# Agent attention and a maxout feed-forward: more turns of queries by transposing DMA, issued in runs, with a fourth slot for four tile classes and a new instruction order

## The chip, the cores and the metric

One Trainium2 chip, one NeuronCore of it. The metric is the device time of one execution in microseconds (us), taken as the median of several runs. One further execution is run under the hardware profiler; the page and the trace come from it. Engines are named as in the profile: PE (TensorE matmul), PEld (TensorE weight load), DVE (VectorE), ACT (ScalarE), POOL (GpSimd), SP (SyncE, which issues the DMAs). "L592" is line 592 of the kernel.

## The reference

```python
def _attn_ref(q, k, v, agents):          # q, k, v: (4, 12544, 128); agents: (4, 49, 128)
    scale = 1.0 / np.sqrt(q.shape[-1])
    def sm(a, b):
        s = scale * (a @ b.transpose(0, 2, 1))
        e = np.exp(s - s.max(-1, keepdims=True))
        return e / (e.sum(-1, keepdims=True) + 1e-09)
    agent_v = sm(agents, k) @ v          # 49 agents gather the values of a batch
    return sm(q, agents) @ agent_v       # each query takes a mix of the agents

def _moe_ref(x, w1, w2, w3, w_out):      # x: (50176, 128); w1, w2, w3: (128, 768); w_out: (768, 128)
    h = np.maximum(np.maximum(x @ w1, x @ w2), x @ w3)
    return h @ w_out                     # float32
```

The attention's result, reshaped to 50176 rows, is the x of the second part.

## The kernel before, in words

**Algebra.** With 49 agents a batch, each query row is a mix of 49 vectors. So the kernel never forms x: it multiplies the 49 agent vectors by the weights once per batch (a tile G) and multiplies the query's exps by G. G holds the differences w3 - w1 and w2 - w1 (columns C31 and C21) and the product w1 @ w_out. Since max(x1, x2, x3) is x1 plus relus of differences, a group's hidden part is two matmuls (`hidden`, L558), a relu on ScalarE (L571) and a maximum on VectorE (L574) for five of six blocks of 128 hidden columns; for block FI = 4 ScalarE does two relus in its place (L565, L568). The output is `out_linear` (L582) plus `out_hidden` (L592) and is divided by the sum of the exps by `out_scale` on VectorE (L599).

**Tiles and stages.** A tile is 128 rows of 128. Queries come in 49 groups (`NQ`): 12 groups of 8 tiles for each of four batches, and group 48 with the 2 tiles left of each. Keys and values come in chunks of 9 tiles (the last of a batch is smaller). Batch 0's keys and values are done first, in a head of some 40 us, together with the weights; those of batches 1 to 3 are done chunk by chunk inside the groups that "host" them (`host_of`: batch 1 in groups 1 to 11, batch 2 in 12 to 22, batch 3 in 24 to 34).

**What a group of queries takes.** `ql` loads it (float32, 512 KB, L513), `qc` casts it to bf16 on POOL into a QB tile (L517), then it is turned (128x128 tiles transposed) into a QT tile. There are two ways: `qt` on TensorE (eight matmuls with the identity, L523) and `qe` on VectorE (L527, out of PSUM); or, for groups in `TURNED`, `qd`, one transposing DMA issued by SP (`turn_by_dma`, L454). Then `sc` (scores, L533), `ex` (exps on ScalarE, L539), `su` and `re` (sums and reciprocals, L545, L550), six times `u`, `a`, `v`, `x` (hidden, relu or maximum), twice `li`, six `p`, `ov` (output), and `st` (store, L607).

**What a hosted chunk takes.** `kl`, `vl` (loads, L325), `kc`, `vc` (casts on POOL to KB and VB tiles, L335), `kt` (a transposing DMA on SP from KB to a KT tile, L454), `ks` (scores, L359), `kx` (exps to an EK tile, L365), `kv` (values, L376), `va` (sum of values on VectorE, L465) and `ea` (sum of exps on POOL, L474). Batch 0's chunks are turned on TensorE instead (L342, L347).

**The weights.** `lwo` loads w_out (L389), `cwo` casts it on POOL (L405), `pl` multiplies w1 by it (L417); all of the output part needs this. `wm` (L382) are warm-up matmuls whose result is not used; `SPARE` is their number.

**Order and slots.** Nothing is scheduled when the kernel is built: the string `ORDER` lists every step, and each engine gets its steps in that order. A word such as `kt1.0/1` names the step and the slot of the tile that it makes. `SLOTS` says how many buffers a tile class has; a step that makes a tile waits until the readers of the tile that had the slot before are done. All DMAs but one are issued by SP in the order of the string, so a DMA that waits holds all behind it; at most eight of them are under way at a time, since each waits for the one eight places ahead.

Of the kernel before, what the change touches and what calls it, by code (L numbers as in the profile page):

```python
# [14 lines left out]
P, H, C, A, B, NT, GT, KT, NF = 128, 64, 128, 49, 4, 98, 8, 9, 6  # L15
# [16 lines left out]
SLOTS = {"UV": 3, "OM": 2, "LD": 13, "QB": 3, "KB": 3, "VB": 4, "KT": 3, "QT": 3, "EQ": 4, "EK": 4, "AS": 3,  # L32
# [8 lines left out]
class Plan:  # L41
# [614 lines left out]
v.0.0/0 kc1.1/2 x.0.0/4 u.0.2/1 gvl v.1.5/2 a.0.2/1 li.0.0/0 kt1.1/2 p.0.0.3 x.1.5/5 p.0.0.1 ex.2/2 u.1.3/0 v.0.2/1 a.1.3/2
p.0.0.5 kt1.2/0 x.0.2/6 ks1.0/1 p.0.0.0 u.1.2/2 kx1.0/1 v.1.3/0 vc1.0/0 a.1.2/0 kl1.3/5 p.0.0.4 x.1.3/7 u.2.5/1 vl1.2/3 p.0.0.2
a.2.5/1 su.1 kl1.4/11 kv1.0 qc.3/0 u.1.1/2 ov.0.0/0 ql.5/9 v.1.2/0 a.1.1/2 vl1.4/2 u.1.4/1 re.1/1 va1.0/0 x.1.2/8 li.0.1/0 qt.3/1
kl1.8/8 vc1.1/0 a.1.4 p.0.1.4 u.1.0/2 qe.3/0 v.1.1/0 qc.4/0 a.1.0/0 v.1.4 x.1.1/2 p.0.1.1 vl1.3/4 p.0.1.5 p.0.1.3 x.1.4/0 p.0.1.2
p.0.1.0 u.2.3/0 ov.0.1 u.2.4/2 a.2.3/2 v.1.0/1 ks1.1/1 x.1.0/4 li.1.0/0 p.1.0.2 a.2.4 su.2 p.1.0.3 p.1.0.5 re.2/0 v.2.5/0 kx1.1/0  # L660
u.2.1/1 v.2.4 x.2.5/6 a.2.1/0 p.1.0.4 kv1.1 p.1.0.1 p.1.0.0 x.2.4/3 va1.1 v.2.1/0 ov.1.0/1 v.2.3/1 vc1.2/0 sc.3/1 x.2.3/1 u.2.2/2
ex.3/0 li.1.1/0 p.1.1.4 kc1.3/1 a.2.2/1 p.1.1.2 x.2.1/0 ks1.2/1 p.1.1.0 v.2.2/1 kx1.2/3 kc1.4/2 u.2.0/2 kt1.3/0 p.1.1.5 x.2.2/4
a.2.0/2 kv1.2 su.3 p.1.1.1 p.1.1.3 kl1.5/11 u.3.5/0 re.3/2 va1.2 v.2.0/1 ov.1.1 vl1.5/5 a.3.5/1 u.3.1/2 li.2.0/1 ql.6/3 x.2.0/7
p.2.0.3 p.2.0.4 kl1.6/6 a.3.1/0 qt.4/0 ql.7/10 u.3.4/0 qe.4/0 kt1.4/2 u.3.3/1 a.3.4 v.3.5/2 p.2.0.5 x.3.5/2 p.2.0.2 p.2.0.0
a.3.3/2 vc1.3/0 p.2.0.1 kl2.1/12 sc.4/0 ov.2.0/2 v.3.4 ex.4/1 v.3.3/2 ea1.0/0 v.3.1/1 x.3.4/5 x.3.3/8 li.2.1/1 vl2.0/7 p.2.1.5
ks1.3/0 su.4 p.2.1.4 kx1.3/1 x.3.1/6 u.3.2/0 u.4.5/2 a.3.2/2 kv1.3 p.2.1.3 kc1.5/1 p.2.1.0 va1.3 re.4/1 v.3.2/1 a.4.5/0 u.3.0/0
x.3.2/7 li.3.0/0 qc.5/0 p.3.0.5 kt1.5/0 a.3.0/1 p.2.1.2 p.2.1.1 u.4.3/2 ov.2.1 ea1.1 v.3.0/1 a.4.3/2 u.4.4/0 vl1.7/9 x.3.0/0
# [196 lines left out]
```

## Time and profile before

| | us |
|---|---|
| median of 3 runs | 447.99 (447.82 to 449.09) |
| the profiled execution | 448.96 |
| its span, first to last instruction | 447.1 |
| DVE maxima L574, 245 of 1219 ns | 293.4 busy |
| ACT relus L571, 245 of 1024 ns | 246.3 busy |
| PE hidden L558 and output L592 | 181.7 and 180.4 busy |
| DVE evictions of turned queries L527, 22 of 684 ns | 15.0 busy |
| PE turns of queries L523, 176 of 228 ns | 14.4 busy |

Busy time is the time in which an engine executes; idle time is split by what ended it. Matmuls are pipelined, so a busy PE may still be waiting. A line of the timeline has start, duration, engine, line, operation, tiles and count, and in brackets the idle time before it and who ended it. The granted clock of TensorE is 1.00 at full speed; the share of DMA is the mean over 16 engines of the time that their packets took, which can exceed 1 when packets overlap.

Transposing DMAs have no size in the profile's issue list; there are 33 of keys (KT<-KB, median 7.0 us from issue to landing) and 27 of queries (QT<-QB, 6.5 us).

### The profile page before, as it was taken

To read this page: it belongs to the slowest core of one execution; us is meant where nothing else is said; L and a number is where in the kernel's file an instruction comes from. 1 tells how busy PE (TensorE), PEld (TensorE's weight loads), DVE (VectorE), ACT (ScalarE), POOL (GpSimd) and SP (SyncE) were. 2 spreads that over 40 slices of the span, in tenths; PEclk is the share of its full clock that TensorE was granted. 3 is DMA by queue.
4 is the path that set the end of the run, shared out by engine and by line. 5 is a ranking of instruction groups with operands and counts; after the bars stand their busy time and mean duration, and the time that the engine had idled before them with its cause. 6 is when DMAs were issued, how large, how long until landed. Compare 5 with 4: busy or idle time off the path is not lost.

```text
span 447.1 us, 12853 instructions
## 1 busy us (share of the span) xinstructions
PE 421.8 (94%) x5260; PEld 270.8 (61%) x5260; DVE 392.1 (88%) x496; ACT 393.6 (88%) x461; POOL 169.5 (38%) x176
## 2 busy tenths in 40 slices
PE   0787899999999999999899999999999999999996
PEld 0554466666666666666566666666665555655675
DVE  1345799999999999999899999998999999999996
ACT  1469799999999999999889999999999999999983
POOL 1641645555694222824871324527601201000000
PEclk9989699999999999999999999999999999999999
DMA  8999999999999999999999999999699464450405
GB/s 312 410 408 387 346 372 281 298 405 308 327 291 307 352 285 285 345 310 225 321 354 253 313 302 345 303 221 353 189 300 282 103 189 122 90 195 22 164 37 202
DMA packets 97045, 121.98 MB, mean 273 GB/s; under 512 B 70423, under 2 KB 73179, under 8 KB 96987
## 3 DMA queue, kind: packets, MB, share of 16 engines
q1 hardware_dynamic: 96784, 121.07, 90.4%
q8 instruction: 41, 0.67, 0.6%
q14 instruction: 17, 0.14, 0.1%
q10 hardware_dynamic: 203, 0.10, 0.1%
HBM read 78.74 MB, written 25.69 MB: 234 GB/s over the span
## 4 chain that ended last, share of the span: by engine, by line
PE 83%; DMA 8%; DVE 3%; issue 2%; POOL 2%; ACT 1%; SPq 1%; DVEq 0%; POOLq 0%
PE UV L558 35%; PE OM L592 31%; PE OM L582 6%; DMA LD<-in_v_dram 4%; PE OM L533 3%; DVE R L574 2%; PE OM L523 2%; DMA LD<-in_k_dram 2%; PE OM L376 2%; PE OM L359 2%; DMA LD<-in_q_dram 1%; PE OM L545 1%; SPq L325 1%; DVE OS L599 1%; POOL QB L517 1%
## 5 line engine op out<-in xcount | busy, mean ns | idle before, releaser
L574 DVE TENSOR_TENSOR R<-UV,AS 128x1024 bf16<-128x1024 f32 x245 | 293.4, 1219 | 17.8 <-PE UV L558 12.9
L571 ACT ACTIVATE AS<-UV 128x1024 bf16<-128x1024 f32 x245 | 246.3, 1024 | 17.8 <-PE UV L558 13.5
L558 PE MATMUL UV<-EQ,G 49*128 49x512 bf16 (+1 forms) x1248 | 181.7, 371 | 0.9
L592 PE MATMUL OM<-wo_bf,R 128*128 128x128 bf16 x2352 | 180.4, 220 | 0.0
L592 PEld LDWEIGHTS <-R 128*128 128x128 bf16 x2352 | 139.8, 98 | 43.4 <-issue 41.1
L558 PEld LDWEIGHTS <-G 49*128 49x128 bf16 x1248 | 61.5, 94 | 61.8 <-issue 21.7
L517 POOL CAST QB<-LD 128x1024 bf16<-128x1024 f32 x49 | 51.1, 1048 | 98.4 <-DMA LD<-in_q_dram 50.3
L335 POOL CAST KB<-LD 128x1152 bf16<-128x1152 f32 (+2 forms) x45 | 49.7, 1116 | 60.4 <-DMA LD<-in_k_dram 42.8
L599 DVE TENSOR_TENSOR OS<-OM,RC 128x512 f32<-128x512 f32 x98 | 67.1, 684 | 3.6 <-PE OM L592 2.5
L335 POOL CAST VB<-LD 128x1152 bf16<-128x1152 f32 (+1 forms) x33 | 37.3, 1137 | 47.7 <-DMA LD<-in_v_dram 14.7
L565 ACT ACTIVATE UV<-UV 128x1024 f32<-128x1024 f32 x49 | 49.8, 1017 | 2.5 <-PE UV L558 1.2
L568 ACT ACTIVATE R<-UV 128x1024 bf16<-128x1024 f32 x49 | 50.1, 1023 | 1.7 <-PE UV L558 1.2
L582 PE MATMUL OM<-G,EQ 128*128 128x256 bf16 x196 | 37.9, 276 | 0.0
L539 ACT ACTIVATE EQ<-OM 128x512 bf16<-128x512 f32 x49 | 29.5, 602 | 0.9 <-PE OM L533 0.6
L474 POOL TENSOR_TENSOR EA<-EA,EK 128x441 f32<-128x441 f32 x27 | 27.6, 1023 | 4.8 <-ACT EK L365 4.1
L347 DVE COPY KT<-UV 128x1152 bf16<-128x1152 bf16 (+1 forms) x12 | 8.2, 700 | 17.3 <-PE UV L342 17.3
L582 PEld LDWEIGHTS <-EQ 128*128 128x128 bf16 x196 | 12.6, 97 | 15.6 <-issue 14.2
L533 PE MATMUL OM<-QT,agT 128*64 128x512 bf16 (+1 forms) x104 | 20.4, 398 | 0.2 <-DMA QT<-QB 0.2
L365 ACT ACTIVATE EK<-OM 128x441 bf16<-128x441 f32 (+1 forms) x33 | 17.8, 540 | 2.9 <-POOL EA L474 1.6
L376 PE MATMUL OM<-EK,VB 128*128 128x49 bf16 x392 | 17.3, 186 | 2.7 <-ACT VB L333 1.4
L359 PEld LDWEIGHTS <-KT 128*128 128x128 bf16 x392 | 14.6, 98 | 7.5 <-issue 4.5
L376 PEld LDWEIGHTS <-VB 128*128 128x128 bf16 x392 | 14.3, 97 | 7.9 <-issue 5.0
(67 smaller groups left out, 186.1 us busy)
## 6 DMA issues: line engine op xcount, KB each, us to landing
LD<-in_q_dram SPq DMA_DIRECT2D x48, 512.0 KB, 6.4
out_dram<-OS SPq DMA_DIRECT2D x48, 512.0 KB, 5.6
LD<-in_k_dram SPq DMA_DIRECT2D x40, 576.0 KB, 7.3
LD<-in_v_dram SPq DMA_DIRECT2D x40, 576.0 KB, 8.7
LD<-in_k_dram SPq DMA_DIRECT2D x3, 512.0 KB, 9.0
LD<-in_v_dram SPq DMA_DIRECT2D x3, 512.0 KB, 8.1
LD<-in_moe_w_dram SPq DMA_DIRECT2D x6, 192.0 KB, 8.4
KT<-KB SPq DMA_TRANSPOSE x33, 7.0
```

The costliest lines, as they stand in the source:

```text
L335: (self.nc.gpsimd if eng == POOL else self.nc.vector).tensor_copy(out=out, in_=src)
L376: self.nc.tensor.matmul(out, vb[:, j, :], e[:, j * A:(j + 1) * A], start=False, stop=True, skip_group_check=True)
L517: return lambda: self.nc.gpsimd.tensor_copy(out=self.t[f"qb.{s}"], in_=self.t[f"q.{s}"][:, :GT, :])
L533: self.nc.tensor.matmul(self.t[f"qs.{s}"][h * H:(h + 1) * H, jj * P:(jj + pairs) * P], self.agT[:, b, :], self.t[f"qT.{s}"][:, 2 * jj + h: ...
L558: self.nc.tensor.matmul(t[:, h, jj * P:(jj + pairs) * P], self.t[f"G{b}"][h * H:h * H + A, c + f * P:c + (f + 1) * P], self.t[f"e.{s}"][h ...
L565: return lambda: self.nc.scalar.activation(self.t[f"u.{s}.{f}"], self.t[f"u.{s}.{f}"], AF.Relu)
L568: return lambda: self.nc.scalar.activation(self.t[f"r.{s}.{f}"], self.t[f"u.{s}.{f}"], AF.Relu)
L571: return lambda: self.nc.scalar.activation(self.t[f"a.{s}.{f}"], self.t[f"u.{s}.{f}"], AF.Relu)
L574: return lambda: self.nc.vector.tensor_tensor(out=self.t[f"r.{s}.{f}"], in0=self.t[f"v.{s}.{f}"], in1=self.t[f"a.{s}.{f}"], op=ALU.max)
L582: self.nc.tensor.matmul(self.t[f"o.{s}.{o}"][:, i * 2 * C:(i + 1) * 2 * C], self.t[f"e.{s}"][:, jj * P:(jj + 1) * P], self.t[f"G{of[jj]}"] ...
L592: self.nc.tensor.matmul(self.t[f"o.{s}.{o}"][:, c:c + C], self.t[f"r.{s}.{f}"][:, h, jj * P:(jj + 1) * P], self.wo_bf[:, f, :], start=Fals ...
L599: self.nc.vector.tensor_tensor(out=self.t[f"os.{s}"][:, j:j + 4, :], in0=self.t[f"o.{s}.{o}"].rearrange("p (j c) -> p j c", c=C), in1=self ...
```

## The change

Four edits, three of them of constants:

- `TURNED` holds all groups from 13 to 48, 36 in place of 27. Groups 14, 16, 18, 20, 22, 24, 28, 30 and 34, which were turned on TensorE and evicted by VectorE, are turned by a transposing DMA on SP.
- QB, KB, KT and QT have four slots each in place of three.
- `SPARE` is 7: one warm-up matmul fewer.
- `ORDER` is new throughout. On SP the transposing DMAs stand in runs: the 69 of them form 24 runs, of up to ten, where 60 formed 43. w_out's load (`lwo`) stands directly behind the load of the second group's queries (`ql.1`), ahead of the first keys of batch 1 (`kl1.0`), where it stood behind those. In the head all of batch 0's keys tend to come before its values.

```diff
-SPARE = 8
+SPARE = 7
...
-TURNED = (*range(13, 36, 2), 26, 32, *range(36, 49))
+TURNED = range(13,49)
...
-SLOTS = {"UV": 3, "OM": 2, "LD": 13, "QB": 3, "KB": 3, "VB": 4, "KT": 3, "QT": 3, "EQ": 4, "EK": 4, "AS": 3,
+SLOTS = {"UV": 3, "OM": 2, "LD": 13, "QB": 4, "KB": 4, "VB": 4, "KT": 4, "QT": 4, "EQ": 4, "EK": 4, "AS": 3,
          "R": 13, "RC": 4, "OS": 9, "G": 4, "VA": 2, "EA": 2, "ES": 2, "KR": 2}
```

The steps on SP, taken out of the two strings, around the end of the head:

```
before: lw2b ql.1 kl1.0 lwo ql.2 kl1.2 ql.4 kl1.1 kt1.0 vl1.0 ql.3 vl1.1 kt1.1 kt1.2 kl1.3 ...
after:  lw2b ql.1 lwo kl1.0 ql.2 kl1.3 ql.3 kl1.1 kl1.2 vl1.1 vl1.0 kt1.0 kt1.1 kt1.3 kt1.2 kl1.9 ...
```

and in groups 16 to 19:

```
before: ql.22 vl2.9 ql.21 qd.19 kt2.7 kl3.1 st.8 vl3.0 vl3.2 kt2.8 kl3.0 vl3.1 kt2.9 qd.21 ql.24 st.14 vl3.5 st.13 kt2.10 kl3.2 ...
after:  ql.24 ql.21 ql.33 ql.22 st.3 st.11 qd.19 kt2.7 qd.20 kt2.8 kt2.9 kt2.10 qd.22 qd.23 kt3.1 qd.21 vl3.5 kl3.8 st.14 ql.29 ...
```

TensorE's steps around the product with w_out:

```
before: u.0.5 qt.1 v.0.1 u.0.4 pl v.0.5 sc.1 v.0.4 qt.2 u.0.0 v.0.3 u.1.5 sc.2 gl ...
after:  u.0.4 v.0.1 qt.1 u.0.3 pl v.0.5 v.0.4 sc.1 v.0.3 gl u.0.0 qt.2 u.1.5 v.0.0 ...
```

More of the change, by code (lines that the diff above doesn't have):

```diff
@@ L720 @@
-u.18.3/0 a.18.3/0 v.17.2/2 x.17.2/5 p.16.1.3 u.17.0/1 a.17.0/1 kt2.8/2 p.16.1.2 kv2.6 va2.6 p.16.1.0 ov.16.1 u.18.5/0 a.18.5/2
-v.17.0/2 u.18.4/1 x.17.0/8 su.18 li.17.0/0 p.17.0.5 p.17.0.3 a.18.4 p.17.0.2 re.18/2 u.18.1/0 v.18.5/2 kl3.0/10 a.18.1/1 v.18.4
-x.18.5/9 p.17.0.1 p.17.0.4 p.17.0.0 x.18.4/6 sc.19/1 qc.22/1 vl3.1/9 ov.17.0/0 v.18.3/0 v.18.1/2 ex.19/1 u.18.2/1 x.18.3/4 vc2.7/2
-li.17.1/0 a.18.2/2 p.17.1.3 p.17.1.0 ks2.7/1 x.18.1/8 su.19 p.17.1.1 kx2.7/3 u.19.5/1 v.18.2/0 a.19.5/0 p.17.1.2 x.18.2/1 u.18.0/2
@@ new lines @@
+u.19.3/0 v.18.0/1 a.19.3/2 u.19.4/2 vl3.5/11 qc.25/3 x.18.0/7 li.18.0/1 p.18.0.1 kl3.8/7 su.19 p.18.0.4 a.19.4 st.14 p.18.0.2
+ea2.7 re.19/1 u.19.1/0 ql.29/6 va2.7 v.19.5/1 a.19.1/0 kl3.0/12 v.19.4 kc3.4/3 x.19.5/4 p.18.0.3 vl3.8/0 p.18.0.5 p.18.0.0
+x.19.4/9 kl3.2/5 sc.20/0 ov.18.0/3 v.19.1/0 v.19.3/1 ex.20/2 st.8 u.19.2/2 x.19.1/6 li.18.1/1 a.19.2/1 ks2.8/0 p.18.1.5 p.18.1.4
+x.19.3/3 su.20 u.20.5/0 kx2.8/1 v.19.2/2 vc3.5/2 ql.28/1 p.18.1.1 a.20.5/0 p.18.1.0 re.20/0 x.19.2/2 u.19.0/1 p.18.1.2 a.19.0/2
@@ new lines @@
+ov.19.1 v.20.0/2 a.21.4 u.21.5/1 ql.26/12 x.20.0/8 su.21 li.20.0/0 p.20.0.3 p.20.0.1 a.21.5/0 p.20.0.2 kl3.5/10 qc.28/1 re.21/1
+v.21.4 v.21.5/2 x.21.4/2 u.21.1/1 x.21.5/3 p.20.0.5 ea2.9 p.20.0.4 ql.32/4 p.20.0.0 a.21.1/2 sc.22/1 ov.20.0/5 fo2/0 v.21.1/0
+v.21.3/2 ex.22/1 qd.24/3 u.21.2/1 x.21.1/9 li.20.1/0 a.21.2/0 p.20.1.4 ks2.10/1 p.20.1.3 x.21.3/7 v.21.2/0 qd.29/0 vc3.0/3
+kx2.10/0 u.22.5/1 p.20.1.5 a.22.5/2 kv2.10 x.21.2/5 u.21.0/2 kt3.0/2 to2 a.21.0/1 su.22 p.20.1.2 re.22/2 u.22.3/1 va2.10 nr2/0,2
@@ new lines @@
+v.21.0/0 a.22.3/0 u.22.4/2 kt3.4/1 x.21.0/4 p.20.1.1 p.20.1.0 li.21.0/1 a.22.4 p.21.0.5 p.21.0.1 qd.25/1 ov.20.1 v.22.5/0 u.22.1/1
+v.22.4 x.22.5/8 a.22.1/1 p.21.0.3 p.21.0.4 kl3.3/11 p.21.0.2 p.21.0.0 x.22.4/6 v.22.1/0 ov.21.0/0 sc.23/0 v.22.3/1 kl3.9/1
+x.22.1/0 ex.23/2 u.22.2/2 li.21.1/1 a.22.2/2 su.23/0 p.21.1.5 p.21.1.1 x.22.3/1 st.15 u.23.5/0 v.22.2/2 a.23.5/1 p.21.1.2 p.21.1.0
+re.23/0 x.22.2/5 gpl2/0 gpa2/1 gvl2 gpc2/0 qc.26/0 gva2 sc.24/0 gvc2 u.22.0/2 p.21.1.3 a.22.0/2 kc3.5/0 p.21.1.4 vl3.1/12 u.23.3/0
@@ new lines @@
+sc.25/1 x.23.0/5 li.23.0/0 qd.27/1 vc3.1/3 p.23.0.3 a.24.4 p.23.0.2 v.24.5/1 u.24.1/0 ex.25/1 x.24.5/2 kc3.2/1 p.23.0.5 p.23.0.4
+a.24.1/2 p.23.0.1 p.23.0.0 v.24.4 kc3.8/2 ov.23.0/8 kt3.2/2 v.24.1/1 u.25.5/0 x.24.4/8 x.24.1/1 li.23.1/1 p.23.1.0 ea3.0/0
+p.23.1.5 a.25.5/1 kt3.3/3 v.24.3/2 u.24.2/1 x.24.3/7 qc.32/3 p.23.1.2 a.24.2/2 ks3.1/0 vl3.9/7 su.25 v.24.2/0 vc3.2/0 ql.34/5
+re.25/2 u.24.0/2 kx3.1/0 x.24.2/6 st.18 p.23.1.4 p.23.1.3 a.24.0/0 kl3.6/4 kv3.1 p.23.1.1 va3.1 u.25.1/1 ql.38/2 ov.23.1 v.24.0/0
@@ new lines @@
+a.25.1/2 v.25.5/2 x.24.0/9 sc.26/0 kl3.10/12 li.24.0/1 p.24.0.2 ex.26/2 u.25.3/1 x.25.5/0 p.24.0.5 kl3.7/8 a.25.3/0 p.24.0.0
+p.24.0.4 u.25.2/0 vl3.4/11 v.25.3/1 a.25.2/1 u.25.4/2 x.25.3/4 p.24.0.1 p.24.0.3 a.25.4 li.24.1/0 p.24.1.0 u.26.5/0 ov.24.0/7
+v.25.1/1 a.26.5/0 v.25.4 x.25.1/9 p.24.1.4 ks3.2/1 p.24.1.3 x.25.4/8 su.26 v.25.2/0 re.26/0 u.25.0/1 x.25.2/7 kx3.2/1 p.24.1.1
+p.24.1.5 a.25.0/2 p.24.1.2 kv3.2 ov.24.1 u.26.4/2 v.25.0/0 a.26.4 u.26.3/1 x.25.0/6 li.25.0/0 p.25.0.1 p.25.0.5 a.26.3/1 p.25.0.3
@@ new lines @@
+kc3.6/3 v.26.4 va3.2 v.26.5/0 x.26.4/2 sc.27/1 x.26.5/1 qc.30/2 p.25.0.0 ql.31/4 p.25.0.4 p.25.0.2 st.23 ex.27/0 u.26.1/2
+ov.25.0/3 u.26.2/1 ql.36/6 a.26.1/0 v.26.3/0 kt3.5/2 ks3.3/1 x.26.3/5 li.25.1/0 p.25.1.2 a.26.2/2 v.26.1/2 p.25.1.0 qd.30/1
+x.26.1/7 p.25.1.5 kx3.3/3 u.26.0/1 v.26.2/0 a.26.0/1 kv3.3 su.27 x.26.2/0 kt3.6/3 u.27.5/2 p.25.1.4 a.27.5/0 p.25.1.1 p.25.1.3
+va3.3 re.27/1 u.27.4/0 ov.25.1 v.26.0/1 a.27.4 u.27.3/2 qc.31/1 x.26.0/4 sc.28/1 li.26.0/0 p.26.0.5 a.27.3/2 p.26.0.2 ea3.1
```

350 lines of the change are left out of this document (165 added, 185 removed).

## The prediction

> **What bounds the kernel now.** I read the page first (busy shares and chain), then the stretches between the exps of neighbouring groups, then the timelines of the two places where TensorE stands still, and last the DMA rate in steps of 1 us.
>
> The page: busy time, and the chain by engine.
>
> ```profile
> PE 421.8 (94%) x5260; PEld 270.8 (61%) x5260; DVE 392.1 (88%) x496; ACT 393.6 (88%) x461; POOL 169.5 (38%) x176
> ...
> PE 83%; DMA 8%; DVE 3%; issue 2%; POOL 2%; ACT 1%; SPq 1%; DVEq 0%; POOLq 0%
> ```
>
> TensorE carries the chain, but its busy time holds waits inside pipelined matmuls. So I look at one group at a time: busy time by stretch, from one group's exps to the next. Columns: stretch and length, then PE, PEld, DVE, ACT, POOL busy, TensorE clock, DMA share, GB/s.
>
> ```profile
> 165.10:173.10 8.00, 8.00 (x110) 5.29 (x108) 7.54 (x11) 7.79 (x10) 2.50 (x3) 1.00 1.12 353
> ...
> 181.30:189.40 8.10, 8.10 (x112) 5.52 (x109) 7.97 (x11) 7.88 (x11) 7.08 (x7) 1.00 1.09 350
> 189.40:197.30 7.90, 7.90 (x104) 5.03 (x101) 7.35 (x10) 7.68 (x11) 3.23 (x3) 1.00 1.13 278
> ...
> 213.50:222.90 9.40, 8.26 (x110) 5.35 (x108) 7.99 (x11) 7.68 (x10) 8.14 (x8) 1.00 1.06 324
> 288.40:296.30 7.90, 7.90 (x104) 5.26 (x101) 7.11 (x10) 7.63 (x11) 0.09 (x1) 1.00 1.17 224
> 296.30:304.20 7.90, 7.90 (x104) 5.04 (x100) 7.45 (x10) 7.65 (x10) 5.00 (x5) 1.00 1.08 314
> ```
>
> The first two stretches hold a turn of queries on TensorE and its eviction on VectorE (L523, L527), the third and the last two do not: theirs came by DMA. VectorE has 0.4 to 0.6 us less to do there, ScalarE the same 7.6 to 7.9 us, and the stretch is hardly shorter. ScalarE, idle 0.2 to 0.3 us in a group, sets the pace with the back-and-forth through three UV slots. The stretch from 213.5 is a stall of 1.4 us.
>
> **The head.** TensorE's timeline:
>
> ```profile
> 45.44 0.49 PE L417 MATMUL OM<-wo_bf,w1T 128*128 128x128 bf16 x6 [1.05 <-POOL wo_bf L405]
> ```
>
> GpSimd's timeline, and the stretches around it (columns as above):
>
> ```profile
> 44.56 0.83 POOL L405 CAST wo_bf<-LD 128x768 bf16<-128x768 f32 x1 [1.39 <-DMA LD<-in_moe_w_out_dram]
> ```
>
> ```profile
> 43.40:47.10 3.70, 2.46 (x24) 1.10 (x21) 2.56 (x4) 2.79 (x5) 2.54 (x3) 1.00 1.02 402
> 47.10:50.50 3.40, 2.98 (x18) 1.24 (x18) 2.12 (x3) 2.41 (x4) 1.93 (x3) 0.50 1.18 262
> 50.50:54.00 3.50, 3.50 (x24) 1.60 (x20) 2.64 (x3) 2.36 (x4) 1.96 (x3) 0.51 1.03 404
> ```
>
> TensorE waits for w_out, is busy 2.46 of 3.70 us, and then has 0.50 of its clock for two stretches.
>
> **The stall.** GpSimd's timeline, then ScalarE's:
>
> ```profile
> 212.34 1.14 POOL L335 CAST KB<-LD 128x1152 bf16<-128x1152 f32 x1 [4.27 <-DMA KT<-KB]
> ...
> 215.52 2.12 POOL L474 TENSOR_TENSOR EA<-EA,EK 128x441 f32<-128x441 f32 x2
> ```
>
> ```profile
> 216.57 0.54 ACT L365 ACTIVATE EK<-OM 128x441 bf16<-128x441 f32 x1 [1.55 <-POOL EA L474]
> ```
>
> A key cast waits 4.27 us for one of three KB slots, which a late transposing DMA still reads; two value casts and the sum of exps queue behind it, and ScalarE waits for the EK slot that this sum frees.
>
> **The DMA queue.** Stretches with POOL busy, clock, DMA share, GB/s:
>
> ```profile
> 200.00:201.00 1.00, 0.00 (x0) 1.00 1.04 417
> ...
> 203.00:204.00 1.00, 1.00 (x2) 1.00 0.38 45
> 204.00:205.00 1.00, 0.51 (x1) 1.00 0.25 59
> ...
> 210.00:211.00 1.00, 0.00 (x0) 1.00 0.12 6
> ```
>
> and the hosting stage beside the early one without transposes (all engines, columns as at first):
>
> ```profile
> 60.00:318.00 258.00, 256.26 (x3317) 167.36 (x3314) 244.31 (x307) 243.97 (x287) 130.72 (x134) 1.00 1.08 310
> 15.00:30.00 15.00, 12.63 (x176) 9.71 (x177) 6.49 (x11) 8.46 (x13) 8.37 (x9) 0.89 1.03 408
> ```
>
> Copies move 400 to 440 GB/s, two transposes in a row 247 and 265 (194 to 196 us), and where a transpose follows copies nearly nothing moves for 1 to 2 us. From 60 to 318 us the share is never under 1: the queue is full.
>
> **The change, part by part.**
>
> The queue: 258 us at 310 GB/s are 80.0 MB. The 44 transposes landed in it (30 of keys, 14 of queries, 32 KB a tile) are 12.4 MB, at 265 GB/s 47 us; the other 67.6 MB at 408 GB/s take 166 us. That leaves 45 us lost in the 34 runs of transposes that the order on SP has there: 1.3 us a run. The new order has, up to the last keys (kt3.10), 13 runs in place of 36, and 55 transposes in place of 47; in the same stretch 12 runs and 51 transposes: 166 + 54 + 16 = 236 us. So the queue gains 22 us of room, although eight more transposes pass it. None of this is on the path while ScalarE sets the pace: 0 us by itself, and it is the cover for all that follows.
>
> Nine turns leave TensorE: eight matmuls (0.62 us in the timeline) and a 684 ns copy on VectorE each (L527: 15.0 us for 22), 5.6 and 6.2 us in all. They go from groups whose limit is ScalarE. The stretches with a turn above take 8.00 and 8.10 us, the late ones without 7.90: 0.13 us each, nine times: -1.2 us. Bounds: 0 (189.4 and 173.1 show no gain for some groups) and ScalarE's whole idle time, 0.29 us each: -2.6. I take the rows. Each adds a transpose on SP, 1.2 to 1.3 us of issue when nothing holds it; SP issues some 260 DMAs in 420 us and has the time.
>
> Four slots for KB, QB, KT, QT: a cast waits one tile later. GpSimd waits 17.4 us in all for KT<-KB and 35.6 for QT<-QB in before's waits; only the one chain above reached ScalarE. I take that stall as gone: -1.4 us. Bounds: -1.4, and +1.4 if one of the same size comes up elsewhere.
>
> w_out is loaded ahead of the first keys of batch 1 in place of behind them: one 576 KB load at 408 GB/s, 1.45 us. Its cast then starts when qc.1 ends on GpSimd (43.2 us, not 44.56), and the product at L417 can start at about 44.1 us, not 45.44. TensorE's own wait was 1.05 us: -1.0 us (0 to -1.4: the cast of qc.2 and its turn, not sooner than 46.4 us, are next late, but the new order puts gl, u.0.0 and v.0.3 ahead of that turn).
>
> The half clock: in it, six hidden matmuls take 1.40 to 1.46 us, later 0.90, eight of L592 1.06 against 0.62; summed over 6.8 us of matmuls that is about 2.5 us. With the wait of 1.05 us gone, the stretch from 43.4 us would be busy some 3.5 of 3.7 us. I take -1.0, between -2.5 (clock stays whole) and +0.5 (another idle stretch of the new head halves it longer). The Trainium skill (TensorE: Matmul & The Clock Gate, Part 1) says that a free-running window of about 3.4 us that counts as idle halves the clock and a busy one restores it. The trace agrees in the step, 6.8 us at 0.50; which share counts as idle no row shows. By the rule alone the term would be 0 or -2.5, and the sum 1 us higher or 1.5 lower.
>
> One warm-up matmul fewer (0.44 us) stands in the wait for the first values: 0. In the new order ScalarE's and VectorE's sequences in the hosting groups keep their pattern (the same seven relus, one exps of keys, five maxima); the last 62 steps of TensorE are the same: 0, with 1 us either way.
>
> Sum: -1.2 - 1.4 - 1.0 - 1.0 = -4.6 us. The profiled execution took 448.96 us (its span 447.1), so 444.4 for such a one; the median of the three runs is 447.99, 0.97 lower: 443.4 us.
>
> **The rivals.**
>
> *SP held by a run (slower).* The new order has a run of ten on SP: qd.19, kt2.7, qd.20, kt2.8, kt2.9, kt2.10, qd.22, qd.23, kt3.1, qd.21. Its fifth keys need the slot that kt2.7's scores in group 19 free, by before's times near 198 us, and the count of the queue puts the run's start near 187. For 10 us no load and no store passes. Against it: the loads up to kl3.4 and ql.24 and the stores up to st.12, but for st.8, stand ahead of the run, so 6 of 9 OS slots are held at its end, and the first value load behind it (vl3.0) is used near 240 us. If a run outlasts this stock, a stall like the one at 213.5 (1.4 us) follows each of the eight runs of four or more: 11 us, near 455 us. It decides from the point where a load behind a run lands later than its cast's turn. Chance 0.07.
>
> *The queue sets the pace (slower).* If runs save nothing, a transpose costs (258 - 166)/44 = 2.1 us each, 51 of them 107 us, and the queue needs 273 us where it had 258: 15 us more, less the 4.6: 458 us. It decides from 3.2 us lost a run ((258 - 166 - 54)/12). Against it, the two in a row at 247 and 265 GB/s. The Trainium skill (VectorE: DVE Perf Modes, Rules for kernel authors) advises TensorE for a 128x128 transpose wherever PSUM will do, and the DMA crossbar otherwise; that rule speaks against moving nine turns off TensorE. Chance 0.04.
>
> *No change.* ScalarE's idle time is the back-and-forth of UV, the clock halves again and the stall moves: 447 to 449 us. Chance 0.10.
>
> *More.* The relieved VectorE also lets ScalarE's idle time fall to nothing and the clock stays whole: 440 us. Chance 0.06.
>
> **How the numbers follow.** The forecast has 0.73. Faster by over 0.3% (1.3 us, about what a measurement of this kernel can tell): 0.73 + 0.06 = 0.79; within: 0.10; slower: 0.07 + 0.04 = 0.11. The terms at their best give -7.9, with 1 us of order 439.0; upwards the range takes in no change, 448.6, and leaves out the two slower cases.
>
> **What would show it.** Right: runs of transposes with one dead stretch each, GB/s higher from 60 to 318 us; no wait of L417 for wo_bf and no half clock near 47 us; no wait of key casts for KT<-KB that ends in ScalarE; stretches of 7.9 us in groups 13 to 35 with ScalarE still at 7.7. Wrong: loads or POOL casts ending TensorE's or ScalarE's waits after a long run; SP waiting for PE with the DMA idle and TensorE short; or unchanged stretches of 8.05 us.

## The result, and the profile after

The changed kernel takes 468.69 us (median of 4 runs, 467.96 to 469.54) against 447.9 us for the kernel before on the same chip: a ratio of 1.0467, interval 1.0429 to 1.0505. The forecast was 443.4 us, with a range of 439.0 to 448.6. The profiled execution took 468.92 us, its span is 467.1.

The page of the changed kernel: busy time, then the chain by engine and by line.

```profile
PE 424.7 (91%) x5187; PEld 269.9 (58%) x5187; DVE 387.4 (83%) x487; ACT 393.5 (84%) x461; POOL 169.1 (36%) x176
...
PE 54%; DMA 18%; POOL 6%; SPq 5%; issue 5%; DVE 4%; ACT 1%; POOLq 0%; DVEq 0%; ACTq 0%
```

ScalarE has the same 393 us of work as before, VectorE 5 us less, and both share a longer span. What changed is the chain: TensorE carried 83% of it, now 54%, and DMA has gone from 8% to 18%, with GpSimd and SP's own issuing behind it. So the engines wait for transfers.

Busy time by stretch in the changed kernel (length, then PE, PEld, DVE, ACT, POOL busy, TensorE clock, DMA share, GB/s). The first three run from one group's exps to the next, the fourth is the hosting stage, the last two are in the head.

```profile
199.20:207.10 7.90, 7.87 (x102) 5.06 (x100) 7.38 (x10) 7.67 (x10) 5.27 (x5) 1.00 1.19 250
176.60:191.30 14.70, 11.07 (x109) 6.37 (x108) 8.31 (x11) 8.60 (x11) 5.00 (x5) 0.77 1.03 419
221.10:233.10 12.00, 9.80 (x122) 6.22 (x122) 8.58 (x10) 9.54 (x12) 6.93 (x8) 1.00 1.02 417
60.00:318.00 258.00, 240.16 (x2977) 152.49 (x2974) 220.45 (x274) 223.95 (x263) 124.62 (x125) 0.97 1.07 316
29.97:36.80 6.83, 5.37 (x72) 4.08 (x73) 1.35 (x2) 5.28 (x9) 2.19 (x2) 0.50 1.03 407
43.40:47.10 3.70, 3.58 (x36) 1.81 (x34) 3.39 (x7) 3.70 (x6) 2.81 (x4) 1.00 1.03 412
```

An undisturbed group such as the one from 199.2 us takes 7.9 us, as forecast. But two groups take 14.7 and 12.0 us (without transposes these two take 8.8 and 9.7, as shown below), with ScalarE idle for 6.1 and 2.5 of them, and in just these the queue moves 417 and 419 GB/s: it is catching up on copies, and the engines wait for them. Such groups stand near 97, 168 to 191, 221 to 250, 285 and 313 us. From 60 to 318 us ScalarE is busy 224 us where it was 244: the 20 us are there.

Waits in the changed kernel (engine and line, what it waited for, us in total, times, longest):

```profile
POOL QB L517 <- DMA LD<-in_q_dram: 65.6, 15, 11.9
POOL KB L335 <- DMA LD<-in_k_dram: 56.0, 15, 12.8
...
POOL VB L335 <- DMA LD<-in_v_dram: 30.2, 10, 8.1
...
POOL QB L517 <- DMA QT<-QB: 25.4, 5, 9.2
...
DVE OS L599 <- DMA out_dram<-OS: 11.2, 6, 3.8
...
PE OM L582 <- DVE OS L599: 8.0, 4, 3.6
...
POOL KB L335 <- DMA KT<-KB: 5.1, 4, 2.8
```

The wait that the change was to relieve fell (KT<-KB, from 17.4 to 5.1 us). New is the wait of L599: VectorE waits 11.2 us for stores that free an OS slot, 0.3 us before. Value casts wait 30.2 us for loads, before 14.7.

One such stall from its start. SP's timeline (the issuing engine's own busy time):

```profile
148.83 9.55 SPq L454 DMA_TRANSPOSE QT<-QB  x2
158.48 2.81 SPq L454 DMA_TRANSPOSE KT<-KB  x2
161.40 3.58 SPq L454 DMA_TRANSPOSE QT<-QB  x2
165.08 3.01 SPq L454 DMA_TRANSPOSE KT<-KB  x2
168.14 1.08 SPq L325 DMA_DIRECT2D LD<-in_k_dram  x2
169.27 0.43 SPq L325 DMA_DIRECT2D LD<-in_v_dram  x1
169.74 0.43 SPq L325 DMA_DIRECT2D LD<-in_k_dram  x1
170.22 1.00 SPq L607 DMA_DIRECT2D out_dram<-OS  x2
```

VectorE's timeline, and ScalarE's:

```profile
180.83 0.69 DVE L599 TENSOR_TENSOR OS<-OM,RC 128x512 f32<-128x512 f32 x1 [3.82 <-DMA out_dram<-OS]
```

```profile
184.67 1.02 ACT L571 ACTIVATE AS<-UV 128x1024 bf16<-128x1024 f32 x1 [5.02 <-PE UV L558]
```

A run of eight transposes holds SP from 148.8 to 168.1 us. Then come four loads, and only then the store of group 1, whose slot the output of group 14 needs. It is issued at 170.8 and lands at 180.7; VectorE's scaling has waited 3.8 us for it, TensorE's next linear product (L582) for that, and ScalarE 5.0 us for TensorE. Part of these 5.0 us is a slower TensorE: while it waits, its granted clock falls to 0.50, from 180.2 to 187.0 us (0.77 on average over the group), and eight matmuls of L592 take 1.04 us there, where twelve take 0.83 before and after. Three more of the stalls have 3.4 us at half clock each (from 105.1, 289.4 and 316.7 us); the kernel before has none from 60 to 318 us. The stall at 97 us is the same with a value load behind a run of four, the one at 221 with a store behind the run of ten.

### The profile page after: what moved, and what is told of

Read it like the earlier page. It is cut to its first block, busy times and chain, and to the rows that moved or that the text cites. A ratio compares the mean times of both kernels' runs of the same rounds, so it can differ in the third digit from the quotient of the medians.

```text
span 467.1 us, 12691 instructions
## 1 busy us (share of the span) xinstructions
PE 424.7 (91%) x5187; PEld 269.9 (58%) x5187; DVE 387.4 (83%) x487; ACT 393.5 (84%) x461; POOL 169.1 (36%) x176
## 4 chain that ended last, share of the span: by engine, by line
PE 54%; DMA 18%; POOL 6%; SPq 5%; issue 5%; DVE 4%; ACT 1%; POOLq 0%; DVEq 0%; ACTq 0%
PE UV L558 22%; PE OM L592 20%; DMA out_dram<-OS 7%; DMA LD<-in_q_dram 5%; PE OM L582 4%; DMA LD<-in_k_dram 4%; SPq L454 2%; PE OM L533 2%; SPq L325 2%; DVE R L574 2%; POOL KB L335 2%; POOL QB L517 2%; DMA LD<-in_v_dram 2%; PE OM L376 1%; POOL VB L335 1%
## 5 line engine op out<-in xcount | busy, mean ns | idle before, releaser
L574 DVE TENSOR_TENSOR R<-UV,AS 128x1024 bf16<-128x1024 f32 x245 | 294.3, 1220 | 24.7 <-PE UV L558 20.5
L558 PE MATMUL UV<-EQ,G 49*128 49x512 bf16 (+1 forms) x1248 | 186.3, 373 | 1.1 <-DVE R L574 0.2
L592 PE MATMUL OM<-wo_bf,R 128*128 128x128 bf16 x2352 | 181.2, 221 | 0.0
L592 PEld LDWEIGHTS <-R 128*128 128x128 bf16 x2352 | 141.3, 99 | 44.8 <-issue 42.2
L517 POOL CAST QB<-LD 128x1024 bf16<-128x1024 f32 x49 | 50.7, 1042 | 91.4 <-DMA LD<-in_q_dram 65.6
L599 DVE TENSOR_TENSOR OS<-OM,RC 128x512 f32<-128x512 f32 x98 | 67.1, 685 | 18.5 <-DMA out_dram<-OS 11.2
L335 POOL CAST VB<-LD 128x1152 bf16<-128x1152 f32 (+1 forms) x33 | 37.3, 1136 | 33.7 <-DMA LD<-in_v_dram 30.2
L582 PE MATMUL OM<-G,EQ 128*128 128x256 bf16 x196 | 38.1, 277 | 8.1 <-DVE OS L599 8.0
L582 PEld LDWEIGHTS <-EQ 128*128 128x128 bf16 x196 | 12.6, 97 | 24.5 <-issue 24.0
L333 ACT ACTIVATE VB<-LD 128x1152 bf16<-128x1152 f32 (+1 forms) x12 | 12.2, 1037 | 17.0 <-DMA LD<-in_v_dram 15.4
L376 PE MATMUL OM<-EK,VB 128*128 128x49 bf16 x392 | 18.4, 191 | 7.6 <-POOL VB L335 3.4
L533 PE MATMUL OM<-QT,agT 128*64 128x512 bf16 (+1 forms) x104 | 20.2, 393 | 1.6 <-DMA QT<-QB 1.4
```

The lines of the kernel that those rows point to most:

```text
L335: (self.nc.gpsimd if eng == POOL else self.nc.vector).tensor_copy(out=out, in_=src)
L376: self.nc.tensor.matmul(out, vb[:, j, :], e[:, j * A:(j + 1) * A], start=False, stop=True, skip_group_check=True)
L517: return lambda: self.nc.gpsimd.tensor_copy(out=self.t[f"qb.{s}"], in_=self.t[f"q.{s}"][:, :GT, :])
L558: self.nc.tensor.matmul(t[:, h, jj * P:(jj + pairs) * P], self.t[f"G{b}"][h * H:h * H + A, c + f * P:c + (f + 1) * P], self.t[f"e.{s}"][h ...
L574: return lambda: self.nc.vector.tensor_tensor(out=self.t[f"r.{s}.{f}"], in0=self.t[f"v.{s}.{f}"], in1=self.t[f"a.{s}.{f}"], op=ALU.max)
L582: self.nc.tensor.matmul(self.t[f"o.{s}.{o}"][:, i * 2 * C:(i + 1) * 2 * C], self.t[f"e.{s}"][:, jj * P:(jj + 1) * P], self.t[f"G{of[jj]}"] ...
```

## Experiments

Ratios are to the kernel before, run on the same chip at the same time, with their 95% intervals.

| kernel | us | ratio |
|---|---|---|
| the changed kernel | 468.69 | 1.0467 (1.0429 to 1.0505) |
| seven more transposes among copies, old order | 455.19 | 1.0137 (1.0105 to 1.0170) |
| the same, copies in due order | 457.59 | 1.0251 (1.0191 to 1.0311) |
| new order, copies in due order | 460.22 | 1.0254 (1.0224 to 1.0285) |
| new order, due order with short runs | 461.92 | 1.0338 (1.0279 to 1.0398) |
| new order, nine transposes as plain copies | 463.82 | 1.0354 (1.0301 to 1.0407) |
| new order, 18 in the long runs as copies | 456.45 | 1.0156 (1.0115 to 1.0197) |
| new order, due order, nine as copies | 455.68 | 1.0151 (1.0113 to 1.0189) |
| new order, all 69 as copies | 443.78 | 0.9916 (0.9892 to 0.9940) |
| old order, all 60 as copies | 446.28 | 0.9966 (0.9939 to 0.9994) |
| old order, w_out sooner | 448.23 | 0.9984 (0.9960 to 1.0008) |
| the same and four slots | 448.90 | 1.0032 (1.0009 to 1.0055) |
| the same and copies in due order | 447.87 | 1.0006 (0.9983 to 1.0029) |

The theories at the start: *order* (needed loads and stores stand behind long runs, the rival "SP held by a run") and *throughput* (a transpose takes about 2 us of a full queue, the rival "the queue sets the pace").

**More transposes without long runs.** In the kernel before, `qt.s` and `qe.s` of seven groups are replaced by one `qd.s` about two groups ahead of its scores. Three of the seven stand alone among the copies; four (groups 14, 16, 20 and 22) stand next to another transpose, and the longest run is three, as before.

```diff
-TURNED = (*range(13, 36, 2), 26, 32, *range(36, 49))
+TURNED = (*range(13, 36, 2), 14, 16, 18, 20, 22, 26, 30, 32, 34, *range(36, 49))
-... "QT": 3
+... "QT": 4
-... qt.14/1 ... qe.14/1 ...
+... qd.14/3 ...
```

> The kernel before, with seven more query groups (14, 16, 18, 20, 22, 30, 34) turned by DMA in place of TensorE, each transpose by itself among the copies, a fourth QT slot for them, nothing else changed. Theory 'throughput' (a transpose costs the full queue about 2 us wherever it stands, (258 - 166)/44 = 2.1 us in the kernel before, 1.85 by the same count in the kernel after): 7 x 2.1 = 14.6 us more queue work, less 7 x 0.13 us of turns, so 460 to 462 us, with no long run in it. Theory 'order' (what costs is that needed loads and stores stand behind long runs of transposes): there are no long runs here, so 447 us, 0.9 us less at best.

455.19 us, 6.1 us more than before: on average about 1 us for each transpose, with the 0.13 us that a turn gave back. Between the two theories: more transposes cost without any run longer than three, but half of what throughput said. The loss is not spread evenly. Most of it is one stall, a group from 173.3 to 187.7 us with ScalarE idle for 6.5: VectorE's scaling (L599) waits 3.9 us for a store, as in the stall above, though only single transposes and pairs stand ahead of that store.

**Copies in due order.** The changed kernel, with its transposes where they were and the loads and stores between them permuted (here, behind the run of eight):

```diff
-kl2.10 kl2.7 vl2.10 kl3.4 st.7 st.1 vl2.7 st.4 ql.20 st.10
+kl2.8 vl2.6 kl2.7 vl2.10 ql.19 st.7 kl2.9 ql.23 ql.22 st.8
```

> The kernel after, with its transposes left where they are in SP's order (the runs of 8 and 10 too), and only the loads and stores between them permuted: at each place of a copy stands the one that is due first, a load by its cast, a store by the output tile that needs its slot. Same transposes, same copies, same bytes. Theory 'order': the waits of output scaling for stores (11.2 us on VectorE) and for late loads go, 20 us in all, and the time is 445 to 450 us. Theory 'throughput': the queue has the same work, so the waits only move to other tiles, and the time stays at 464 to 469 us.

460.22 us. 2.1% (1.0467 to 1.0254), 9.5 us, come back: neither theory's number. The waits of this kernel:

```profile
POOL QB L517 <- DMA QT<-QB: 61.2, 11, 16.8
...
POOL KB L335 <- DMA KT<-KB: 40.7, 8, 7.7
...
POOL KB L335 <- DMA LD<-in_k_dram: 23.2, 11, 7.0
...
POOL QB L517 <- DMA LD<-in_q_dram: 9.0, 3, 7.3
...
PE OM L533 <- DMA QT<-QB: 7.5, 2, 4.2
```

The waits for loads shrink (query loads from 65.6 to 9.0 us), the one for stores is gone, and in their place casts and scores wait for transposes (L533, 7.5 us). Whatever goes first, something else is late.

**The queue alone.** No computation; SP issues loads of 512 KB and transposes of 256 KB in five patterns.

> No computation at all: SP's queue alone, with loads of 512 KB, transposes of 256 KB (8 tiles), in five stages of 48 DMAs: copies only; then 32 copies and 16 transposes as copy, copy, transpose; then the same in runs of four; then in runs of eight; last 32 transposes alone (before these, 49 loads each stored again). 32 copies at 408 GB/s take 41 us. The prediction's own count (0.99 us a transpose at 265 GB/s and 1.3 us a run): 16 transposes take 36.6 us in singles (78 us in all), 21 us in runs of four (62), 18.4 in runs of eight (59.5). Theory 'throughput' (2.1 us each wherever it stands): 33.6 us, 75 us in all three. Theory 'paced by issue' (in a run SP needs about 1.35 us to issue each, whatever the queue could do): 21.6 us plus a switch a run, 65 to 68 us in runs, and the transposes alone 1.35 us apart, 43 us for 32.

Stretches from the last landing of one stage to the last of the next (columns: length, DVE and POOL busy, clock, DMA share, GB/s): copy-copy-transpose; runs of four; runs of eight (16 transposes and 32 copies each); 32 transposes alone.

```profile
287.33:343.48 56.15, 0.00 (x0) 0.00 (x0) 1.00 1.10 372
343.48:405.71 62.23, 0.00 (x0) 0.00 (x0) 1.00 1.05 334
405.71:468.95 63.24, 0.00 (x0) 0.00 (x0) 1.00 1.03 333
468.95:512.77 43.82, 0.00 (x0) 0.00 (x0) 1.00 1.00 188
```

A copy takes 1.28 us in the stage of copies, 32 of them 41.0. So a transpose costs 0.95 us by itself among copies, 1.33 in runs of four, 1.39 in runs of eight, 1.37 alone: runs make it dearer. SP's timeline shows why, a single and a run of eight:

```profile
286.11 1.06 SPq L78 DMA_DIRECT2D ld<-in_q_dram  x2
287.22 2.69 SPq L80 DMA_TRANSPOSE dst<-src  x1
...
418.42 17.01 SPq L92 DMA_TRANSPOSE dst<-src  x8
435.47 13.24 SPq L90 DMA_DIRECT2D ld<-in_q_dram  x16
```

Behind eight copies the first transpose holds SP for 5.4 us and the second for 3.3, until only a few DMAs are left ahead of it, and each further one for 1.3 us; the run of eight keeps SP for 17.0 us though it costs the queue about 11. After it, the first copy lands 2.2 us behind the last transpose, not 1.28. The prediction's own count had singles dearest, 78, 62 and 59.5 us for the three patterns; they took 56, 62 and 63, in the opposite order. The 32 transposes alone took 43.8 us, as "paced by issue" said (43).

**Busy engines, stores, casts.** The same, for why it is 1.6 us in the kernel (by landings from 60 to 318 us, the transposes and the copy right behind each run take 1.68 us a transpose more than those copies would at 408 GB/s in the kernel before, 1.59 in the changed one; the landing is the time at which a DMA's semaphore is full, and each DMA is given the time since the landing ahead of it).

> SP's queue alone again, for one question: a transpose between copies took 0.87 us there, and about 1.6 (with the copy behind it) in the whole kernels. Stages: 18 loads and then copy, copy, transpose 14 times, while TensorE, ScalarE, VectorE and GpSimd work on tiles of their own; the same with the engines idle; then with each transpose reading a tile that GpSimd casts from a load four rounds old; then load, store, transpose 14 times; then copy, transpose 14 times. If busy engines slow a transpose: 1.5 us or more each in the first stage and 0.87 in the second. If stores do: in the fourth. If it is SP's waits in the kernel (a transpose lets no more than three DMAs stand ahead of it): 0.9 in all stages where the casts are early, and more where SP waits for a cast.

14 rounds a stage, from the last landing ahead of the first round to the last of the stage: copy-copy-transpose with busy engines, with idle ones, with the source cast by GpSimd, load-store-transpose, copy-transpose (columns: length, PE, PEld, DVE, ACT, POOL, clock, DMA share, GB/s).

```profile
27.39:81.06 53.67, 53.67 (x250) 24.36 (x249) 52.23 (x43) 52.05 (x52) 50.63 (x49) 1.00 1.13 335
104.68:153.18 48.50, 0.00 (x0) 0.00 (x0) 0.00 (x0) 0.00 (x0) 3.13 (x3) 0.50 1.10 373
153.18:201.67 48.49, 0.00 (x0) 0.00 (x0) 0.00 (x0) 0.00 (x0) 11.46 (x11) 0.50 1.09 379
201.67:255.70 54.03, 0.00 (x0) 0.00 (x0) 0.00 (x0) 0.00 (x0) 0.00 (x0) 0.50 1.10 340
255.70:292.39 36.69, 0.00 (x0) 0.00 (x0) 0.00 (x0) 0.00 (x0) 0.00 (x0) 0.50 1.12 293
```

With the copies at 1.28 us, a transpose costs 1.27 us beside busy engines, 0.90 beside idle ones, 0.90 with casts, 1.30 with stores in the round, 1.34 when every other DMA is one. (The 0.87 us in the expectation is 0.95 by the whole stage of copy-copy-transpose above.) Busy engines do not slow every transpose: 12 of the 14 land 0.80 to 0.98 us behind the DMA ahead of them, as all 14 do beside idle engines, and the 5.2 us between the two stages are in a few late landings near 53 to 61 and at 80 us, whose cause no run shows. With stores, the load behind the transpose lands late, 1.8 us or more in seven of the 14 rounds. Busy engines and stores make 0.36 and 0.40 us each, so 1.6 with both is plausible; but no stage had both, and none had a full queue of loads and stores without transposes, so why it is 1.6 stays open.

**All transposes as copies.** One line, in the changed kernel and in the kernel before:

```diff
-            self.nc.sync.dma_start_transpose(out=self.t[f"{dst}{r}"][:, :n, :],
-                                             in_=self.t[f"{src}{r}"][:, :n, :].rearrange("p j c -> p (j c)"))
+            self.nc.sync.dma_start(self.t[f"{dst}{r}"][:, :n, :], self.t[f"{src}{r}"][:, :n, :])
```

> The kernel after, where each of its 69 transposing DMAs is a plain copy of the same tile at the same place in SP's order (the tiles arrive unturned, so scores are of other numbers; all else is as in the kernel after). If the transposes' time in the queue is the whole cause: a copy of 256 KB takes about 0.65 us where a transpose took 1.6, some 48 us less queue work from 60 to 318 us, and the time is what the prediction's other terms give, 442 to 446 us. If the new order is bad for the engines by itself: 452 us or more, with waits that name no DMA.

> The kernel before, where each of its 60 transposing DMAs is a plain copy of the same tile at the same place (scores of other numbers). If transposes cost the kernel before nothing on its path, because ScalarE and the UV slots set its pace: 446 to 448 us. If they already cost it something (the stall at 213.5 and such): 440 to 445 us, and fewer transposes are the direction of a faster kernel.

443.78 and 446.28 us. The new order with plain copies is where the forecast was (443.4). That the 69 DMAs transpose is the whole loss, 5.5% (0.9916 to 1.0467), 24.7 us; the order does not lose time without them. A plain copy of a tile is shorter in the queue and also holds SP for 0.57 us in place of 2.3 (mean of the 69), so these two costs are not told apart here. The page's chain by engine, and the hosting stage of that kernel:

```profile
PE 85%; DVE 4%; ACT 2%; issue 1%; DVEq 0%; ACTq 0%
```

```profile
60.00:318.00 258.00, 257.45 (x3273) 165.42 (x3269) 241.37 (x302) 245.91 (x291) 136.02 (x139) 1.00 0.88 333
```

No DMA is left in the chain, and the DMA share, 1.07 with transposes, is 0.88. The kernel before loses only 0.34% to its transposes, 1.5 us.

**Which transposes.** The same line behind a condition: the nine added queries, in the changed kernel and in the one with copies in due order; and the 18 transposes of the two longest runs.

```diff
+            if src == "qb." and r in (14, 16, 18, 20, 22, 24, 28, 30, 34):
...
+            if r in (15, 16, 17, 18, 19, 20, 21, 22, 23, "2.3", "2.4", "2.5", "2.6", "2.7", "2.8", "2.9", "2.10", "3.1"):
```

> The kernel after, where only the nine transposes of the queries that the change adds (groups 14, 16, 18, 20, 22, 24, 28, 30, 34) are plain copies at the same place; the other 60 stay (these nine groups have scores of other numbers). Theory 'count': nine times about 1 us less queue work and shorter holds of SP, so 455 to 460 us, and more than half of the loss stays with the order. If the nine are the straw on a full queue: 447 to 451 us.

> The kernel after with loads and stores in due order (460.2 us when run) and the nine added transposes as plain copies (these nine groups have scores of other numbers): as many transposes as in the kernel before, in runs, with copies in due order. If order of the copies and number of transposes are the two causes: 447 to 451 us. If runs cost by themselves: 454 to 457 us.

> The kernel after, where only the 18 transposes of the two longest runs (8 and 10) are plain copies at the same place (their tiles arrive unturned); the other 51 stay, among them five of the nine added. Per transpose, the nine as copies gave back 4.9 of 25 us, 0.54 each. If a transpose costs the same wherever it stands: 18 x 0.54 = 10 us less, 458 to 460. If what costs is that loads and stores stand behind a long run: these two runs are followed by the stalls near 177, 221 and 242 us, 13 to 15 us in all, and the time is 452 to 456 us.

463.82, 455.68 and 456.45 us. The nine are 1.1% (5.1 us) by the new order, 1.0% (4.6 us) by the due order: the two causes, number and order, add up. The 18 are 3.1%, 13.9 us, 0.77 us each against 0.56; copies in their place take away the long runs and 18 transposes at once. And the groups behind the long runs are whole again; of the kernel with the 18 as copies, the stretches that answer to 176.60 and 221.10 above:

```profile
175.20:184.00 8.80, 8.80 (x112) 5.42 (x110) 8.23 (x11) 8.59 (x11) 3.11 (x3) 1.00 1.03 419
213.70:223.40 9.70, 9.67 (x122) 6.20 (x122) 9.03 (x11) 9.49 (x12) 6.46 (x9) 1.00 1.03 419
```

14.7 and 12.0 us have become 8.8 and 9.7, while the stalls behind the shorter runs stay (ScalarE idle 5.3 us near 97 us, 3.7 near 272).

**Short runs, and due order without them.** SP's order of the changed kernel between groups 5 and 37 written by due time, transposes too, with a copy behind each where one may go (from there on no run is longer than three); then the kernel with seven more transposes, with its copies in due order.

> The kernel after, with SP's order from group 5 to group 37 written anew: the first due goes first, transposes too (by the scores that need them), and after a transpose a copy where one may go, so that transposes stand in ones and twos and no run is longer than two. Same steps on all other engines, same 55 transposes. In the queue alone a transpose between copies took 0.87 us and one in a run 1.36. Theory 'runs cost': 45 or so transposes are 0.5 us cheaper, 22 us of queue, and the time is 445 to 450 us. Theory 'count' (in the whole kernel the transposes of before, mostly singles, and of after, mostly in runs, cost the same 1.6 us each): no better than the due order with runs, 457 to 463 us.

> The kernel before with seven more queries by DMA among the copies (455.2 us when run), now with its loads and stores permuted so that at each place of a copy the one due first stands; transposes where they were. Theory 'order': the 6 us lost there were one store that came late (the stall near 177 us), and the time is 446 to 448 us. Theory 'count': seven transposes are about 7 us of work that a full queue has no room for, and the time stays at 452 to 456 us.

461.92 and 457.59 us. Singles are cheaper in the queue alone and not in the kernel: by landings a transpose takes 1.56 us in the first, in 42 runs, and 1.58 in the due order with its 12 runs. In the first, casts wait 59.2 us for QT<-QB and scores 7.4; in the second 63.2 and 2.3. Due order did not help the second: it is 1.1% slower than with the copies where they were (1.0137 to 1.0251). The wait for a store is gone there, but ScalarE idles 2.8 and 4.5 us in the groups from 181.6 and 192.2 us, where scores (L533) wait 2.3 us for a late transpose. So the 9.5 us that due order gave belong to the changed kernel's order and are no general rule. The first does not tell what runs cost by themselves, since the transposes' own order changed too; the two show that even without long runs this number of transposes keeps the kernel over 455 us.

**The other parts of the change.** Swapping two words and two slots (`lwo`, `kl1.0`), then four slots for KB, QB, KT, QT, then due order:

> The kernel before, with only w_out loaded ahead of the first keys of batch 1 in place of behind them (the two trade places and slots). The prediction's terms: 1.0 us of TensorE's wait and 1.0 us of the half clock, so 446 us. Rival: the DMA queue of the stage behind it sets when that stage ends, and the head's gain is lost there: 447.5 to 448.5.

> The kernel before with two parts of the change and neither its order nor its transposes: w_out ahead of the first keys, and four slots each for KB, QB, KT and QT, given out in turn. The prediction's terms: -1.4 us for the stall at 213.5 (a key cast waits for a KB slot) beside -1 to -2 of the head: 445 to 446 us. Rival: the cast that no longer waits is followed by a load or a transpose as late as it was, and only the head's 0.9 us is left: 448 us.

> The kernel before with w_out sooner, the four slots, and its loads and stores permuted by when they are due; its own 47 transposes to kt3.10 where they were. If the kernel before lost time to copies out of turn too: 443 to 445 us. If ScalarE and the UV slots set its pace: as with the slots alone, 445 to 448 us.

448.23, 448.90 and 447.87 us: w_out alone may be the forecast's 1.0 us (its interval takes in no change), the rest is no gain. No version that turns all its tiles is clearly faster than the kernel before; the two that are leave the turning out.

## Why the prediction was wrong, step by step

**The step that failed: "45 us lost in the 34 runs of transposes ... 1.3 us a run", and from it "22 us of room".** The count was of one kernel, and the loss could be shared out by runs, by transposes, or partly to copies; I shared it by runs because GB/s falls where a transpose follows copies. By landings, the kernel before lost 19 us of it between one copy and the next, and the rest goes with the number of transposes: 1.68 us each there, 1.59 in the changed kernel, with 34 and 12 runs, and 1.56 with 42 short ones. In the queue alone a run of eight costs 1.39 us each and a single 0.95. So gathering transposes made almost no room: in the same 258 us the changed kernel's queue lands 51 transposes and 66.7 MB of copies, the kernel before 44 and 67.5 MB (so seven of the eight more fall in that stretch). Nor is the DMA share "never under 1" there: the prediction's own lines have 0.12 to 0.38 in single microseconds, and only stretches of 15 us, up to 315 us, are all at 1.00 or more. "0 us by itself" and "the cover for all that follows" fell with it: the queue was on the path, behind both long runs.

The Trainium skill (Advanced Engine Details and Errata, X-Bar Transpose (TRN2)) says that transposing DMAs are as fast as ordinary ones, with 350 to 400 GB/s expected. The runs do not agree: 32 in a row move 188 GB/s where copies move 408 or more, and the cheapest, 256 KB in 0.90 us among copies and beside idle engines, comes to 290.

**"1.2 to 1.3 us of issue when nothing holds it; SP ... has the time."** In the trace, SP's 69 transposes take 160 us, 2.3 us each, because each stays in issue until few DMAs are ahead of it. But the 60 of the kernel before took 171 us, 2.9 each, and the order with short runs 188, so the hold is not longer for the runs. SP's total time was beside the point; what counts is which load or store stands behind a transpose when it is due.

**The rival "SP held by a run"** is what the stall traced above shows, and plain copies in place of the two longest runs give back 13.9 of the 24.7 us. Its mechanism was described rightly, and put aside with two numbers that did not hold. The run of ten was to start near 187 us and last 10; it ran from 195.4 to 216.0. And the stock was checked for the run of ten alone: at the run of eight, the store of group 1 stood behind it. Its price, 1.4 us a run, was taken from one stall of the kernel before; the stalls here cost up to 6.1 us of ScalarE, 24 in all. The other rival, 2.1 us for each transpose, had the size in the queue (1.6) nearer than the forecast, but the time does not follow the queue one for one: of the 24.7 us, 5 are the nine added, about 9.5 are copies out of turn, and some 9 are left for the old 60 transposes standing where they do in the new order (10.5 us in 1.0151 against 0.9916, and 1.5 in the old order). Whether run length or the place of the transposes makes those 9 stays open.

The Trainium skill (VectorE: DVE Perf Modes, Rules for kernel authors) advises TensorE for a 128x128 transpose wherever PSUM will do. The runs agree: nine turns cost about 5 us by DMA, and by the stretches of before 1.2 on TensorE.

**What held.** Groups without a stall take 7.9 us with no turn in them. TensorE's wait for w_out at L417 is gone, and the cast starts at 43.56 us instead of 44.56 (the product itself starts at 45.66, not at the forecast's 44.1, behind other work of TensorE):

```profile
43.56 0.83 POOL L405 CAST wo_bf<-LD 128x768 bf16<-128x768 f32 x1
```

The stretch from 43.40 us is busy 3.58 of 3.70, as forecast. The half clock did not go but moved, to 6.83 us at 0.50 from 29.97 (fifth line of the stretches above); still, group 3's exps start at 64.0 us instead of 65.7. Not all of that is the change: the kernel with seven more transposes has the head of the kernel before, and in its trace no half clock falls near 47 us (3.4 us from 30.4) and these exps start at 64.5. So the half clock that the forecast took 1.0 us off for is not in every execution. Of 62 executions of the kernel before, the nine with a mean clock of 0.987 to 0.989 have a median of 450.3 us, the 18 with 0.998 or more 447.7; the profiled one had 0.988. Part of the 0.97 us from that execution to the median may therefore be the same half clock, taken off twice. With every transpose a copy, new order against old order is 0.9916 to 0.9966, 2.2 us, where the terms for turns, w_out and clock say 3.2; no run takes the terms for turns and clock by themselves, so that 443.78 is so near 443.4 is in part luck. The stall term (1.4 us, KB slots) gave nothing: the group at 213.5 us takes 8.1 us in place of 9.4 with four slots, but also with w_out sooner alone and three slots, and the time does not fall; with four slots ScalarE idles 1.4 us instead in each of the groups from 121.2 and 129.5 us (1.0 and 0.8 before).

## What to carry to other kernels

A transfer that holds its issuing engine is paid by everything queued behind it: before gathering such transfers, list what stands behind each of them and when it is due, at every run and not at the longest one. A loss counted once in one kernel fits several laws (per switch, per transfer, per wait); a run of the queue alone, in two patterns, can refute one (here the loss per run), and one with the costly transfers made plain tells whether they are the cause at all. And a full queue gives no cover: what was added to it here made something else late.

## What was not expected of the hardware

A transposing DMA of 256 KB holds SP for 1.2 us at least, and for 5.4 us behind eight copies; when its issue ends, mostly one to four DMAs are still ahead of it in these traces, where a copy is issued with up to seven ahead. The same transpose takes 0.90 us of the queue among copies with idle engines, 1.27 on average with busy ones, 1.30 among stores, and 1.37 in a row.
